# Loading a tile's queries by one transfer of 2 KB rows instead of two transfers of 1 KB rows

## The chip, the cores and the metric

The kernel runs on one core of one Trainium2 chip. The metric is device time in microseconds (us) for one execution. Three executions of the kernel before took 438.06, 438.45 and 440.13 us; their median, 438.45 us, is the time before. One further execution was profiled: 438.54 us, with a span of 436.9 us from its first to its last instruction.

## The reference

A decayed linear attention ("retention") is followed by a mixture of eight experts. `q`, `k` and `v` are fp32 arrays of 4 batches x 8 heads x 768 tokens x 64 values.

```python
for b in range(nb):                       # blocks of 64 tokens, in order
    intra = einsum('bhic,bhjc->bhij', qb, kb) * Dmask   # lam ** (i - j), i >= j
    intra = einsum('bhij,bhjd->bhid', intra, vb)
    inter = einsum('bhid,bhde->bhie', qb * lam_pow, kv_state)
    out[:, :, sl] = intra + inter
    kv_state = lam_block * kv_state + einsum('bhsd,bhse->bhde', kb_dec, vb)
# then, with x = the 3072 x 512 rows of out:
e_idx = argmax(x @ w_gate, axis=1)        # one expert per row
out[row] = gate * eom * (relu(x @ w1[e]) @ w2[e])
```

## The kernel before, in words

The work has two stages. In the first, the attention runs over 24 tiles: a tile is 128 tokens of one batch with all eight heads, and the four batches of one stretch of 128 tokens follow each other. In the second, the rows are gathered expert by expert and go through `w1` and `w2`.

For a tile `n`, `load_qkv` (line 145) brings three blocks of 256 KB from HBM, all issued by SP (SyncE): the keys in two transfers (line 171), the queries in two (line 165), the values in one (line 173). Keys and values land with one token per partition, so their contiguous pieces are one head's 64 values, 256 bytes. The queries land in another way: a partition holds four successive tokens of one head, 1 KB that is contiguous in HBM. One transfer brings heads 0 to 3 into columns 0 to 255 of the tile, the other heads 4 to 7 into columns 256 to 511. Partition `4s + m` of the first holds tokens `4s` to `4s+3` of head `m`.

`stage_a` (line 312) turns keys and queries over on TensorE: four 128x128 transposes of the keys into the PSUM bank `pk`, four of the queries into `pq` (line 325). ScalarE then copies `pk` to `kT` in one instruction (line 328) and `pq` to `qT` in four, each of 64 partitions x 256 elements (line 330). It is these four copies that put the tokens back in order: `query_parts` (line 303) gives for each copy the elements of `pq` it reads and the places in `qT` it writes, every second column. After `stage_a`, `qT` has the same layout whatever way the queries came in. `stage_b` (line 347) multiplies `kT` and `qT` into the banks `ps`, VectorE applies the decay (line 368), `stage_c1` and `stage_c` multiply with the running state (line 383) and with the values (line 400) and update the state (line 413). ScalarE takes the result to `xT` (line 407), VectorE turns it to rows `xn` (line 475), and SP writes those to the DRAM buffer `x_d` (line 477), from which the experts gather later (line 769).

The order of the instructions on each engine is the order of the code (a schedule written out by hand). In step `s` of the loop at line 1054, SP is given the keys and queries of a tile five to seven steps ahead, the values of a tile two less ahead, and then the `x_d` write of tile `s - 1`; GpSimd (POOL) forms `qd` (line 339) and the decayed keys `kd` (line 300). Tiles 0 to 15 land in eight buffers that the expert weights use later; those of tiles 18 to 21 land in a shared pool of 44 slots, which also holds `kT`, `qT`, `xT` and `xn`. A slot that held `xn` is free when its `x_d` write has landed. SP works through its transfers in that order, one after the other, with nothing else in between.

The pieces of the code that the steps below touch:

Of the kernel before, what the change touches and what calls it, by code (L numbers as in the profile page):

```python
# [23 lines left out]
def kernel(  # L24
# [13 lines left out]
    nc = tc.nc  # L38
    B, H, S, D = q.shape
# [3 lines left out]
    NPAIR = H // 2  # L43
# [31 lines left out]
    def slot(name, dtype=F32):  # L75
        return pool.tile([P, 512], dtype, tag="slot", bufs=NSLOT, name=name)
# [68 lines left out]
    def load_qkv(n, i0=0, i1=3):  # L145
        if n >= NTILE:
            return
        c, b = divmod(n, B)
        ts = qkv.setdefault(n, [])
        if n not in packs:  # L150
            if n < EARLY + 2:
                tag, bufs = (("whi", 4), ("wlo", 4))[n % 2] if n < EARLY else ("raw", 3)
                t = wpool.tile([P, 4, 512], F32, tag=tag, bufs=bufs, name=f"qkv_{n}")
                packs[n] = [t[:, i, :] for i in range(4)]
            elif n >= NTILE - 2:
                ts2 = [pool.tile([P, 8 * P], F32, tag="wide", bufs=4, name=f"qkv_{n}_{i}") for i in range(2)]
                packs[n] = [t[:, 512 * i : 512 * i + 512] for t in ts2 for i in range(2)]
        for i, (nm, src) in list(enumerate((("k", k), ("q", q), ("v", v))))[i0:i1]:
            t = packs[n][i] if n in packs else slot(f"{nm}_{n}")
            rows = src[b, :, c * P : (c + 1) * P, :]  # L160
            if nm == "q":

                rows = rows.rearrange("(y m) (s r) d -> y s m (r d)", y=2, r=4)
                for j in range(2):
                    nc.sync.dma_start(t[:, 256 * j : 256 * j + 256], rows[j])
            else:
                t = t.rearrange("p (h d) -> p h d", h=H)
                rows = rows.rearrange("h t d -> t h d")
                if nm == "k":
                    for y in range(2):  # L170
                        nc.sync.dma_start(t.rearrange("p (m y) d -> p y m d", y=2)[:, y], rows[:, 4 * y : 4 * y + 4])
                else:
                    nc.sync.dma_start(t, rows)
            ts.append(t)


    with tc.manual_schedule():
        lamb = const.tile([P, H], F32, name="lamb")
        nc.scalar.dma_start(lamb, lam.rearrange("(o h) -> o h", o=1).broadcast_to([P, H]))
        load_qkv(0, 0, 2)  # L180
        blank = const.tile([P, 512], BF16, name="blank")
        nc.gpsimd.memset(blank, 0.0)
        warm = const.tile([P, 1], F32, name="warm")
        nc.gpsimd.memset(warm, 0.0)
        idle = bank("idle")

        def keep_warm(count):
            for _ in range(count):
                nc.tensor.matmul(idle, blank[:, 0:P], blank, start=True, stop=True)

        keep_warm(7)
        nc.scalar.activation(out=warm, in_=warm, func=AF.Exp)
        ident = const.tile([P, P], F32, name="ident")
        make_identity(nc, ident)
        decay = pool.tile([P, H, P], F32, tag="decay", name="decay")
        load_qkv(1, 0, 2)
        wgs = const.tile([P, NKC, EG], F32, name="wgs")
        nc.gpsimd.memset(wgs, 0.0)
        load_qkv(0, 2, 3)
        for n in range(2, AHEAD):  # L200
            load_qkv(n, 0, 2)
            if n == 2:
                nc.sync.dma_start(wgs[:, :, 0:E], w_gate.rearrange("(c p) e -> p c e", p=P))
                nc.sync.dma_start(wgs[:, :, E : 2 * E], w_output_gate.rearrange("(c p) e -> p c e", p=P))
            else:
                load_qkv(n - 2, 2, 3)
# [96 lines left out]
    def query_parts(pq):  # L303
        for j in range(2):
            for o in range(2):
                yield (
                    slice(j * D, (j + 1) * D),
                    lambda t, o=o: t.rearrange("p g (s i o) -> p g s i o", i=2, o=2)[:, :, :, :, o],
                    pq[o * D : (o + 1) * D, 256 * j : 256 * j + 256].rearrange("p (i s g) -> p g s i", i=2, g=NPAIR),
                )  # L310

    def stage_a(n):
        c, b = divmod(n, B)
        k_in, q_in = qkv[n][0:2]
        pk = bank(f"pk_{n}")
        pq = bank(f"pq_{n}")
        for src, dst in ((k_in, pk), (q_in, pq)):
            if n < 2 and (n > 0 or dst is pq):
                keep_warm(1)
            if dst is pq:  # L320
                src = src.rearrange("p (m y d) -> p m y d", y=2, d=D)
            else:
                src = src.rearrange("p (m y) d -> p m y d", y=2)
            for m in range(4):
                nc.tensor.transpose(out=dst[:, m * P : (m + 1) * P], in_=src[:, m], identity=ident)  # L325
        kT = slot(f"kT_{n}").rearrange("p (g t) -> p g t", g=NPAIR)
        qT = slot(f"qT_{n}").rearrange("p (g t) -> p g t", g=NPAIR)
        nc.scalar.copy(out=kT, in_=pk.rearrange("p (g t) -> p g t", g=NPAIR))
        for r, view, src in query_parts(pq):
            nc.scalar.copy(out=view(qT[r]), in_=src)  # L330
        live[n] = dict(kT=kT, qT=qT, qd=None, kd=None)
# [708 lines left out]
    with tc.manual_schedule():  # L1040
# [181 lines left out]
        for p in range(E):  # L1222
# [3 lines left out]
            rows = p not in TURNED  # L1226
# [41 lines left out]
            for i, j in enumerate(steps):  # L1268
# [10 lines left out]
                m = max(ns - 1, 1)  # L1279
# [108 lines left out]
```

## Time and profile before

| | |
|---|---|
| Median of three executions | 438.45 us (438.06 to 440.13) |
| Profiled execution, its span | 438.54 us, 436.9 us |
| TensorE busy (matmul) | 401.5 us, 92% of the span |
| VectorE, ScalarE, GpSimd busy | 285.5, 188.0, 235.7 us |
| Transfers issued by SP's queue | 88240 packets, 62.40 MB |
| First and last issue of queries by SP | 1.9 us, 98.6 us |

The attention stage fills about the first 120 us: the last copy to `qT` starts at 119.7 us. In the rows of the trace, PE is TensorE, DVE is VectorE, ACT is ScalarE, POOL is GpSimd, SPq is the queue of SP in which it issues transfers; L165 is line 165 of the kernel. "DMA share" is the mean busy share of the 16 engines that carry the transfers, 1.00 when all 16 have a packet under way all the time. A busy TensorE is not a TensorE at its peak, since matmuls are pipelined.

### The profile page before, as it was taken

How to read it: one execution, taken by the hardware profiler on the slowest of the kernel's cores; microseconds unless marked ns; L12 is line 12 of the kernel's file. 1: busy time of each engine (PE TensorE's matmuls, PEld its weight loads, DVE VectorE, ACT ScalarE, POOL GpSimd, SP SyncE). 2: the span in 40 equal slices, each digit the busy share in tenths (PEclk: the TensorE clock that was granted, in tenths of full speed). 3: DMA queues.
4: the chain of work that ended last, by engine and by line, in shares of the span. 5: the costliest groups of instructions: out<-in, count | busy, mean ns of one | idle time of the engine just before them, and what ended most of it. 6: DMA issues, size and time to landing. Idle time of an engine off the chain costs nothing.

```text
span 436.9 us, 10421 instructions
## 1 busy us (share of the span) xinstructions
PE 401.5 (92%) x3816; PEld 366.4 (84%) x3816; DVE 285.5 (65%) x822; ACT 188.0 (43%) x455; POOL 235.7 (54%) x284
## 2 busy tenths in 40 slices
PE   8999899788366989979999999999999999999993
PEld 4888789677355969669999999999999989989983
DVE  3757768394587853485967966886785774874610
ACT  5766576355423602254604613532642552542400
POOL 4276866655485287758668366366376446311011
PEclk9999999999695999999999999999999999999998
DMA  7989898989672135565447945965964876361001
GB/s 171 219 241 242 213 249 215 246 227 263 188 216 76 49 95 203 160 199 183 132 158 209 298 144 170 290 220 151 292 221 131 266 247 216 128 202 60 1 28 50
DMA packets 95471, 79.42 MB, mean 182 GB/s; under 512 B 59564, under 2 KB 71856, under 8 KB 95408
## 3 DMA queue, kind: packets, MB, share of 16 engines
q1 hardware_dynamic: 88240, 62.40, 48.8%
q0 software_dynamic: 7024, 16.24, 11.9%
q8 instruction: 32, 0.52, 0.5%
q14 instruction: 31, 0.25, 0.2%
q10 hardware_dynamic: 144, 0.00, 0.0%
HBM read 62.45 MB, written 16.55 MB: 181 GB/s over the span
## 4 chain that ended last, share of the span: by engine, by line
PE 68%; DMA 11%; DVE 8%; SPq 4%; issue 4%; POOL 3%; ACT 1%; POOLq 0%; DVEq 0%; ACTq 0%
PE ph_None L80 9%; PE ph_None L81 9%; PE ph_None L79 9%; PE py L79 5%; PE py L81 5%; PE py L80 5%; DMA xg<-x_d,rows 4%; PE pyr L80 3%; PE pyr L79 3%; PE pyr L81 3%; PE po L400 3%; PE ps L359 2%; DMA index<-tab_d 2%; DMA qkv<-in_k_dram 2%; DVE wlo L133 2%
## 5 line engine op out<-in xcount | busy, mean ns | idle before, releaser
L769 POOL DMA_INDIRECT xg<-x_d,rows x103 | 114.2, 1109 | 77.3 <-issue 32.3
L133 DVE TENSOR_TENSOR wlo<-raw,whi 128x512 fp32r<-128x512 f32 x128 | 87.7, 708 | 0.6 <-ACT whi L124 0.6
L836 ACT ACTIVATE hhi<-ph_None 128x400 fp32r<-128x400 f32 (+4 forms) x56 | 28.1, 501 | 116.9 <-PE ph_None L81 112.1
L79 PE MATMUL ph_None<-xhi,whi 128*128 128x400 f32 (+4 forms) x224 | 76.3, 341 | 2.2 <-ACT xhi L800 2.2
L80 PE MATMUL ph_None<-xlo,whi 128*128 128x400 f32 (+4 forms) x224 | 76.3, 341 | 0.3 <-DVE xlo L804 0.3
L81 PE MATMUL ph_None<-xhi,wlo 128*128 128x400 f32 (+4 forms) x224 | 76.2, 340 | 0.0
L124 ACT CAST whi<-raw 128x512 fp32r<-128x512 f32 x128 | 74.4, 615 | 3.1 <-DMA raw<-in_moe_w_dram 3.1
L837 DVE SCALAR_TENSOR_TENSOR hlo<-ph_None,hhi 128x400 fp32r<-128x400 f32 (+4 forms) x56 | 31.8, 567 | 33.9 <-ACT hhi L836 31.9
L368 DVE TENSOR_TENSOR at<-ps,decay 128x512 f32<-128x512 f32 x48 | 31.5, 686 | 27.0 <-PE ps L359 21.7
L79 PEld LDWEIGHTS ph_None<-xhi,whi 128*128 128x128 f32 x224 | 42.0, 188 | 3.1 <-ACT xhi L800 2.7
L80 PE MATMUL py<-hlo,whi 128*128 128x400 f32 (+2 forms) x128 | 44.5, 348 | 0.0
L81 PE MATMUL py<-hhi,wlo 128*128 128x400 f32 (+2 forms) x128 | 44.5, 348 | 0.0
L79 PE MATMUL py<-hhi,whi 128*128 128x400 f32 (+2 forms) x128 | 44.5, 348 | 0.0
L80 PEld LDWEIGHTS ph_None<-xlo,whi 128*128 128x128 f32 x224 | 42.1, 188 | 1.0 <-DVE xlo L804 0.6
L81 PEld LDWEIGHTS ph_None<-xhi,wlo 128*128 128x128 f32 x224 | 42.1, 188 | 0.3
L330 ACT COPY qT<-pq 64x256 f32<-64x256 f32 x96 | 37.6, 391 | 7.5 <-PE pq L325 6.6
L953 POOL DMA_INDIRECT out_dram<-yn,table x12 | 12.7, 1058 | 49.9 <-DVE yn L1013 32.6
L81 PE MATMUL pyr<-whi,hlo 128*128 128x512 f32 (+2 forms) x96 | 37.5, 391 | 0.2 <-DVE hlo L837 0.2
L80 PE MATMUL pyr<-wlo,hhi 128*128 128x512 f32 (+2 forms) x96 | 37.5, 391 | 0.0
L79 PE MATMUL pyr<-whi,hhi 128*128 128x512 f32 (+2 forms) x96 | 37.5, 390 | 0.0
L800 ACT CAST xhi<-y 128x256 fp32r<-128x256 f32 (+3 forms) x64 | 19.8, 362 | 38.7 <-DVE y L786 30.3
L612 POOL DMA_INDIRECT tab_d<-rec,idx x24 | 24.9, 1039 | 18.7 <-issue 11.2
(179 smaller groups left out, 762.3 us busy)
## 6 DMA issues: line engine op xcount, KB each, us to landing
raw<-in_moe_w_dram SPq DMA_DIRECT2D x29, 1024.0 KB
qkv<-in_k_dram SPq DMA_DIRECT2D x40, 128.0 KB
qkv<-in_q_dram SPq DMA_DIRECT2D x40, 128.0 KB
qkv<-in_v_dram SPq DMA_DIRECT2D x20, 256.0 KB
x_d<-xn SPq DMA_DIRECT2D x20, 256.0 KB
raw<-in_moe_w_dram POOLq DMA_DIRECT2D x3, 1024.0 KB, 5.8
yd<-yo SPq DMA_DIRECT2D x12, 256.0 KB
yr<-yd SPq DMA_DIRECT2D x48, 64.0 KB
```

What stands on the lines that cost most here:

```text
L79: nc.tensor.matmul(ps, a[0], b[0], start=first, stop=False)
L80: nc.tensor.matmul(ps, a[0], b[1], start=False, stop=False)
L81: nc.tensor.matmul(ps, a[1], b[0], start=False, stop=last)
L124: nc.scalar.copy(out=hi, in_=src)
L133: eng.tensor_tensor(out=lo, in0=src, in1=hi.bitcast(F32), op=ALU.subtract)
L330: nc.scalar.copy(out=view(qT[r]), in_=src)
L368: nc.vector.tensor_tensor(out=at, in0=ps.rearrange("p (g t) -> p g t", g=NPAIR), in1=dec[:, j], op=ALU.mult)
L612: nc.gpsimd.indirect_dma_start(out=tab_d, out_offset=bass.IndirectOffsetOnAxis(ap=idx, axis=0), in_=rec, in_offset=None, bounds_check=P * ...
L769: nc.gpsimd.indirect_dma_start(out=xg[(p, b // 4)][:, (b % 4) * P : (b % 4 + 1) * P], out_offset=None, in_=x_q[0 : 4 * rows], in_offset=ba ...
L800: nc.scalar.copy(out=hi, in_=src)
L836: nc.scalar.activation(out=hi[:, r], in_=ph[:, r], func=AF.Relu)
L837: nc.vector.scalar_tensor_tensor(out=lo[:, r], in0=ph[:, r], scalar=0.0, in1=hi[:, r].bitcast(F32), op0=ALU.max, op1=ALU.subtract,)
```

## The change

The two transfers become one. A partition now holds eight successive tokens of one head, 2 KB that is contiguous in HBM: partition `16h + s` holds tokens `8s` to `8s+7` of head `h`. The source is walked as 8 heads, 16 pieces in each, 512 elements in each piece; before it was 32 pieces, 4 heads, 256 elements, once for each half of the heads. The transposes are the same four instructions; what their columns mean is different, and so `query_parts` reads `pq` in another order. The copies remain four of 64x256 and write the same elements of `qT` in the same order, every second column.

```diff
             if nm == "q":
 
-                rows = rows.rearrange("(y m) (s r) d -> y s m (r d)", y=2, r=4)
-                for j in range(2):
-                    nc.sync.dma_start(t[:, 256 * j : 256 * j + 256], rows[j])
+                nc.sync.dma_start(t, rows.rearrange("h (s r) d -> h s (r d)", r=8))
...
             for o in range(2):
                 yield (
                     slice(j * D, (j + 1) * D),
-                    lambda t, o=o: t.rearrange("p g (s i o) -> p g s i o", i=2, o=2)[:, :, :, :, o],
-                    pq[o * D : (o + 1) * D, 256 * j : 256 * j + 256].rearrange("p (i s g) -> p g s i", i=2, g=NPAIR),
+                    lambda t, o=o: t.rearrange("p g (s m o) -> p g s m o", m=4, o=2)[:, :, :, :, o],
+                    pq[o * D : (o + 1) * D].rearrange("p (m y g s) -> p y g s m", m=4, y=2, g=NPAIR)[:, j],
                 )
```

On TensorE, VectorE, ScalarE and GpSimd the instructions stand in the same order and number. On SP, 24 transfers are gone. The head of SP's queue, before (the number behind `qkv` is the buffer of a tile; the last figures are partitions and elements, and `x2` stands for two equal transfers):

```order
L171 DMA qkv_78<-in_k_dram 128x4x64 x2
L165 DMA qkv_78<-in_q_dram 128x1x256 x2
L171 DMA qkv_102<-in_k_dram 128x4x64 x2
L165 DMA qkv_102<-in_q_dram 128x1x256 x2
L173 DMA qkv_78<-in_v_dram 128x8x64
```

and now (the lines stand two higher, and the buffers have other numbers):

```order
L169 DMA qkv_78<-in_k_dram 128x4x64 x2
L163 DMA qkv_78<-in_q_dram 128x1x512
L169 DMA qkv_101<-in_k_dram 128x4x64 x2
L163 DMA qkv_101<-in_q_dram 128x1x512
L171 DMA qkv_78<-in_v_dram 128x8x64
```

Nothing changes places; everything behind a tile's queries comes one transfer earlier for each tile ahead of it. Further on, in step 6, where the keys and queries of two tiles are issued together, before:

```order
L171 DMA qkv_808<-in_k_dram 128x4x64 x2
L165 DMA qkv_808<-in_q_dram 128x1x256 x2
L171 DMA qkv_813<-in_k_dram 128x4x64 x2
L165 DMA qkv_813<-in_q_dram 128x1x256 x2
L173 DMA qkv_571<-in_v_dram 128x8x64
L173 DMA qkv_700<-in_v_dram 128x8x64
L477 DMA x_d<-xn_873 128x512
```

and now:

```order
L169 DMA qkv_797<-in_k_dram 128x4x64 x2
L163 DMA qkv_797<-in_q_dram 128x1x512
L169 DMA qkv_801<-in_k_dram 128x4x64 x2
L163 DMA qkv_801<-in_q_dram 128x1x512
L171 DMA qkv_562<-in_v_dram 128x8x64
L171 DMA qkv_690<-in_v_dram 128x8x64
L475 DMA x_d<-xn_860 128x512
```

The values of tiles 9 and 10 and the `x_d` write stand behind two query transfers in place of four.

## The prediction

> **What bounds the kernel now.** I read first the windows by stage, to see which stage the queries' transfers lie in and whether another could give time back. Columns are the stretch, its length, the busy time of each engine, the granted TensorE clock, the mean busy share of the 16 transfer engines, and GB/s.
>
> ```profile
> 0.00:22.00 22.00, 19.48 (x274) 14.45 (x274) 11.96 (x36) 13.94 (x33) 7.65 (x42) 1.00 0.83 195
> 22.00:82.00 60.00, 56.33 (x1246) 49.84 (x1245) 42.05 (x147) 35.08 (x94) 42.91 (x45) 1.00 0.89 233
> 82.00:110.00 28.00, 22.84 (x500) 19.47 (x498) 15.01 (x53) 15.55 (x43) 14.68 (x15) 1.00 0.93 248
> 0.00:110.00 110.00, 98.65 (x2016) 83.76 (x2016) 69.02 (x234) 64.58 (x170) 65.24 (x101) 1.00 0.89 229
> 140.00:436.90 296.90, 284.99 (x1573) 268.10 (x1570) 194.31 (x515) 112.94 (x255) 152.09 (x164) 0.99 0.52 167
> ```
>
> From 140 us on TensorE works 285.0 of 296.9 us: a delay of the attention reaches the end undiminished, and time won there is won at the end. In the first 110 us two resources are near full together: TensorE, 98.65 us, and the transfer engines, 0.89 x 110 = 97.9 us, so 12.1 us are free on the average transfer engine.
>
> Next the timeline of SP's queue, its start and one steady piece (start, length, line, transfers).
>
> ```profile
> 0.92 0.99 SPq L171 DMA_DIRECT2D qkv<-in_k_dram  x2
> 1.95 1.29 SPq L165 DMA_DIRECT2D qkv<-in_q_dram  x2
> 3.28 1.14 SPq L171 DMA_DIRECT2D qkv<-in_k_dram  x2
> 4.46 1.19 SPq L165 DMA_DIRECT2D qkv<-in_q_dram  x2
> 5.69 0.60 SPq L173 DMA_DIRECT2D qkv<-in_v_dram  x1
> ...
> 34.06 1.90 SPq L171 DMA_DIRECT2D qkv<-in_k_dram  x2
> 36.01 1.21 SPq L165 DMA_DIRECT2D qkv<-in_q_dram  x2
> 37.26 0.59 SPq L173 DMA_DIRECT2D qkv<-in_v_dram  x1
> 37.95 0.52 SPq L477 DMA_DIRECT2D x_d<-xn  x1
> 38.57 1.92 SPq L171 DMA_DIRECT2D qkv<-in_k_dram  x2
> ```
>
> SP issues without a pause; a tile took it 38.57 - 34.06 = 4.5 us there, of which the two query transfers are 1.2. So SP is a third full resource. What this costs is in the table of waits (engine and line, what it waited for, total, times, longest), for 0 to 110 us, and in the long steps of the chain that ended last:
>
> ```profile
> POOL kd L300 <- DMA qkv<-in_k_dram: 4.7, 1, 4.7
> PE po L400 <- DMA qkv<-in_v_dram: 3.0, 2, 1.9
> ACT xT L407 <- DMA x_d<-xn: 2.0, 1, 2.0
> ACT kT L328 <- DMA x_d<-xn: 1.7, 1, 1.7
> PE pq L325 <- DMA qkv<-in_q_dram: 0.6, 2, 0.5
> PE pk L325 <- DMA qkv<-in_k_dram: 0.4, 1, 0.4
> ```
>
> ```profile
> 17.19 5.10 DMA qkv<-in_k_dram
> 31.88 4.71 DMA qkv<-in_q_dram
> 77.55 5.26 DMA x_d<-xn
> 106.52 7.41 DMA index<-tab_d
> ```
>
> TensorE waits only 3.0 + 0.6 + 0.4 = 4.0 us for transfers in 110, but each of k, q, v and the `x_d` write stands in the chain at some point: they arrive just in time, with no stock. Whatever slows transfers is felt soon.
>
> **The change, part by part.** *The issues.* 48 query transfers become 24. A query transfer holds SP for 0.60 us, a key transfer for 0.56:
>
> ```profile
> L165 SPq DMA_DIRECT2D qkv<-in_q_dram x40: 540/602/1788, 1.9 to 98.6; - x40
> L171 SPq DMA_DIRECT2D qkv<-in_k_dram x40: 367/558/1826, 0.9 to 97.1; - x40
> ```
>
> 24 x 0.60 = 14.4 us of SP's time go. What they are worth depends on whether SP can use them: at the start it can, since the engines are still empty. Tile 1's keys, for which POOL waits 4.7 us, are behind one query issue fewer, tile 2's behind two: I take the latter, 2 x 0.65 = 1.3 us of the start. Later the gain has a ceiling, the 4.0 us of TensorE's waits, and is had only if the transfers themselves do not become slower.
>
> *The transfers.* They do, I think. The bytes are the same, 256 KB a tile. But the outermost count of the source falls from 32 to 8, while every other large load of SP has an outermost count that is a multiple of 16 (128 partitions). How a transfer is dealt out shows in the ACT queue's single transfer, the 128 rows of `lamb`:
>
> ```profile
> q10 hardware_dynamic: 144, 0.00, 0.0%
> lamb<-in_lam_dram ACTq DMA_DIRECT2D x1, 4.0 KB
> ```
>
> 144 packets are 128 rows and 16 more, one for each engine, so its outer rows were dealt to all 16. Eight outer rows can be dealt to no more than eight engines unless they are cut further, which no row here shows. My forecast is that the new query transfer runs on eight.
>
> The Trainium skill ("DMA: Bandwidth & Descriptors", section "Why a DMA increments its semaphore by 16 and not by 1") says that the number of engines is the largest one up to 16 that divides the slowest dimension of both sides, and that the queue of SP takes the lowest-numbered ones. By that rule it is 8, always the same eight; no run here has shown a transfer with fewer than 16, and without the rule the sum would be that of the second rival.
>
> The price of a tile's queries on one engine, from two stretches in which the expert weights come in rows of 2 KB and more:
>
> ```profile
> 105.00:107.00 2.00, 1.28 (x48) 1.04 (x40) 0.00 (x0) 1.94 (x6) 0.00 (x0) 1.00 1.00 294
> 243.00:246.00 3.00, 3.00 (x17) 2.98 (x17) 2.83 (x7) 2.39 (x7) 0.00 (x0) 1.00 1.02 403
> ```
>
> Per engine that is 294 / 1.00 / 16 = 18.4 and 403 / 1.02 / 16 = 24.7 GB/s. 262144 bytes on eight engines then take 1.78 or 1.33 us, and I take 1.40, nearer to the fast end because half the engines leave memory to the others. Before, on 16 engines in 1 KB pieces, the dearest price is the average of the stage, 229 / 0.89 / 16 = 16.1 GB/s, or 1.02 us, the cheapest 24.7 GB/s, or 0.66; I take 0.75, since 1 KB lies nearer to 2 KB than to the 256-byte rows that make the average. Each of the eight loaded engines so gets 0.65 us more a tile, between 0.31 (1.33 - 1.02) and 1.12 (1.78 - 0.66). Over 24 tiles: 15.6 us, between 7 and 27. The other eight get less work, which helps nobody, because a transfer of keys or values has landed only when its last engine has.
>
> *The sum.* The loaded engines have 97.9 + 15.6 = 113.5 us of work where 110 were available: 3.5 us too much. They also cannot start before about 2 us, when the first packets follow the first issue at 0.92: 5.5. The start gains 1.3: +4.2, and of this a little is lent by packets that overlap (a share of 1.02 above), so +4.0. On the profiled run's 438.54 us this is 442.5; its distance to the median, 0.1 us, is nothing here. SP then waits for room in its queue instead of issuing, so the waits of TensorE for values and queries grow in place of shrinking, behind them `ps`, VectorE's decay and ScalarE's `xT`, which all follow TensorE; and the `x_d` writes, on whose landing ScalarE waits 3.7 us for free slots, come later too.
>
> *The copies.* ScalarE reads `pq` with the same large step (128 columns) innermost, four times in a row instead of twice, and writes as before. The nearest rows are the strided copies of today and a copy of the same length without a stride:
>
> ```profile
> L330 ACT COPY qT<-pq 64x256 f32<-64x256 f32 x96 | 37.6, 391 | 7.5 <-PE pq L325 6.6
> L407 ACT COPY xT<-po 128x256 f32<-128x256 f32 x48 | 16.8, 373 | 12.8 <-PE po L400 7.9 <-DMA x_d<-xn 2.0 <-PE pq L325 1.7
> ```
>
> All the striding costs 18 ns a copy, so a change of it is bounded by 96 x 0.018 = 1.7 us either way, on an engine that is busy 64.58 of 110 us: nothing. Without that cover, as in the few places where the chain runs through `qT`, it is 0.07 us a tile. The transposes have the same shapes: nothing.
>
> **The rivals.** *Eight engines, absorbed (same).* Break-even is where the added load fits into the 12.1 free us less the 2 of the start: 10.1 / 24 = 0.42 us a tile. That is inside my bounds (0.31 to 1.12): it holds if the old price was near 1.0, or if the two-fold shorter issue lets SP fill the gaps that the engines have today while queries are issued. For it: the free 12 us are an average and can be used. Against it: the chain's landings of 5 us show queues that already build up. It gives 438.5.
>
> *Sixteen engines (faster).* If the eight rows are cut further and dealt to all, the load stays (0.66 to 0.89 us a tile against 0.66 to 1.02) and SP's 14.4 us are a plain gain: TensorE's 4.0 us of waits go, and 1.3 of the start: 438.5 - 5.3 = 433 at best, 434.5 with some wait left. Against it is the count of 8.
>
> *Eight engines, and one of them already the last (much slower).* The engines carry more than data:
>
> ```profile
> q8 instruction: 32, 0.52, 0.5%
> ```
>
> 32 packets of 16 KB hold one engine each for some 0.66 us at 24.7 GB/s. TensorE has 2016 of its 3816 matmuls before 110 us, so about 17 of them, 11 us, fall there. If they go always to one engine, it has 97.9 + 11 = 109 of 110 us today, which would explain why single SP issues take up to 1.8 us. If that one is among the eight, no reserve is left: it decides from the first tile, and 15.6 - 1.3 - (1 free us) = 13 us would be lost, of which the slack between tiles may give back a few: 449.
>
> **How the numbers follow.** What a measurement of this kernel can tell from no change is 0.5%, 2.2 us: under 436.3 is faster, over 440.6 slower. Chances: forecast 0.48, with its own range 440 to 447; absorbed 0.22; sixteen engines 0.16; the last engine 0.14. Faster: 0.16 and 0.06 of the absorbed case, whose start may gain: 0.22. Same: the other 0.16 and 0.07 of the forecast's lower end: 0.23. Slower: 0.41 + 0.14 = 0.55. The time is that of the likeliest, 442.5. The range takes in sixteen engines as far as 434 and the last engine as far as 451.
>
> **What would show it.** In the section on queues, SP's queue has 88240 packets; 6144 of 1 KB give way to 3072 of 2 KB. If each engine that takes part adds one closing packet, 48 x 16 of these go, and 24 x 8 come with eight engines or 24 x 16 with sixteen: 84592 or 84784. The bytes stay at 62.40 MB. In the forecast the waits `po L400 <- in_v_dram` and those for `in_q_dram` and `in_k_dram` grow from 4.0 us to about 8, SP has issues of well over 0.6 us at the values and keys that follow queries, and the last `qT` copy starts near 124 us, not 119.7. If SP runs ahead, these waits vanish and the copy starts before 117, the transfers were not slowed, and the step on the eight engines is wrong. If `qT` takes other than 0.39 us, the step on the copies is. If the attention ends as forecast but the whole does not, the windows after 140 us will show that they gave time back, against what I read there.

## The result, and the profile after

The changed kernel took 441.31 us (median of six executions, 440.83 to 443.95), the kernel before 437.96 us beside it. The ratio is 1.0096, with a 95% interval of 1.0067 to 1.0125: 3.35 us slower, more than can be taken for no change. The profiled execution took 441.37 us, its span is 439.7 us against 436.9.

The windows by stage of the kernel after (columns as in the prediction):

```profile
0.00:22.00 22.00, 16.14 (x206) 10.77 (x206) 9.25 (x29) 11.39 (x27) 6.95 (x41) 1.00 0.83 163
22.00:82.00 60.00, 57.60 (x1262) 50.43 (x1266) 43.69 (x150) 38.35 (x101) 40.47 (x42) 1.00 0.96 233
0.00:110.00 110.00, 96.03 (x1918) 80.79 (x1919) 70.06 (x234) 63.34 (x164) 63.78 (x100) 0.98 0.92 215
140.00:439.70 299.70, 287.56 (x1589) 270.67 (x1585) 197.39 (x524) 113.34 (x257) 154.25 (x165) 0.99 0.52 166
```

Within 110 us 1918 matmuls are on record, not 2016, and 215 GB/s come in, not 229, while the transfer engines show *more* busy time: 0.92, not 0.89. The start is hurt most: in the same 22 us 163 GB/s instead of 195. The granted clock does not explain it: its mean is 0.976 over this execution and 0.977 over the one before, and up to 82 us it is 1.00 in both. After 140 us nothing is given back: TensorE works 287.6 of 299.7 us there, as densely as before.

SP's queue in the section on queues and, below it, its timeline at the start (start, length, line, transfers) after the change:

```profile
q1 hardware_dynamic: 84592, 62.39, 50.3%
```

```profile
0.92 1.00 SPq L169 DMA_DIRECT2D qkv<-in_k_dram  x2
1.97 0.78 SPq L163 DMA_DIRECT2D qkv<-in_q_dram  x1
2.79 0.96 SPq L169 DMA_DIRECT2D qkv<-in_k_dram  x2
3.79 0.64 SPq L163 DMA_DIRECT2D qkv<-in_q_dram  x1
4.47 0.46 SPq L171 DMA_DIRECT2D qkv<-in_v_dram  x1
4.97 2.31 SPq L169 DMA_DIRECT2D qkv<-in_k_dram  x2
7.33 2.76 SPq L163 DMA_DIRECT2D qkv<-in_q_dram  x1
```

84592 is the count that the prediction worked out for eight engines. For two tiles SP is ahead: the first values are issued at 4.47 us, before at 5.69. Then the keys of tile 2 hold SP for 2.31 us and its queries for 2.76 us, and the lead is gone. Nor did the lead bring anything earlier. The landings of the keys of tile 1 stand in both chains that ended last (start, length), first before, then after:

```profile
3.91 2.83 DMA qkv<-in_k_dram
```

```profile
3.25 4.79 DMA qkv<-in_k_dram
```

They were issued 0.66 us earlier and landed 1.30 us later, at 8.04 us and not at 6.74. The rows of single operations (minimum, median, maximum in ns, first and last start in us; the row of queries is without tiles 18 to 21) show that a long issue is no exception:

```profile
L163 SPq DMA_DIRECT2D qkv<-in_q_dram x20: 621/1396/2759, 2.0 to 102.2; - x20
L328 ACT COPY qT<-pq x96: 375/393/426, 7.7 to 122.9; 64x256 f32<-64x256 f32 x96
```

One issue of queries has a median of 1396 ns, more than the two of 602 ns that it replaces. Medians leave out the few long issues, though. Added up from the timelines, all 48 issues of queries before held SP for 34.7 us, the 24 after for 31.5: of the 14.4 us that were to be saved, 3.2 are. More than that goes at the `x_d` writes, whose issues come to 22.4 us instead of 14.7 (before, then after):

```profile
L477 SPq DMA_DIRECT2D x_d<-xn x22: 337/524/2117, 24.1 to 145.1; - x22
L475 SPq DMA_DIRECT2D x_d<-xn x22: 337/946/2499, 26.1 to 148.2; - x22
```

The copies are as long as before, and the last starts 3.2 us later (119.7 before).

The table of waits after the change, 0 to 110 us:

```profile
ACT kT L326 <- DMA x_d<-xn: 5.0, 2, 4.1
PE pq L323 <- DMA qkv<-in_q_dram: 4.9, 6, 1.4
ACT qT L328 <- DMA x_d<-xn: 3.8, 1, 3.8
ACT xT L405 <- DMA x_d<-xn: 1.7, 1, 1.7
PE po L398 <- DMA qkv<-in_v_dram: 0.8, 1, 0.8
PE pk L323 <- DMA qkv<-in_k_dram: 0.3, 1, 0.3
```

TensorE waits for transfers 4.9 + 0.8 + 0.3 = 6.0 us (4.0 before): for queries 4.9 instead of 0.6, for values 0.8 instead of 3.0. ScalarE, which needs the slots that an `x_d` write sets free, waits 5.0 + 3.8 + 1.7 = 10.5 us, where it was 3.7. Two landings of queries stand in the chain that ended last (start, length); the longest landing of queries in the chain before took 4.71 us:

```profile
23.38 6.64 DMA qkv<-in_q_dram
...
42.61 6.93 DMA qkv<-in_q_dram
```

How the delay grows is seen from when TensorE begins to turn over the keys of tiles 2, 5, 11, 17 and 23. The timeline of TensorE, first the kernel before, then after:

```profile
11.70 0.66 PE L325 MATMUL pk<-ident,qkv 128*128 128x128 f32 x4
...
22.43 0.63 PE L325 MATMUL pk<-ident,qkv 128*128 128x128 f32 x4 [0.38 <-DMA qkv<-in_k_dram]
...
49.19 0.66 PE L325 MATMUL pk<-ident,qkv 128*128 128x128 f32 x4
...
76.51 0.66 PE L325 MATMUL pk<-ident,qkv 128*128 128x128 f32 x4
...
115.82 1.09 PE L325 MATMUL pk<-ident,qkv 128*128 128x128 f32 x4 [7.28 <-issue]
```

```profile
13.79 0.66 PE L323 MATMUL pk<-ident,qkv 128*128 128x128 f32 x4
...
25.21 0.66 PE L323 MATMUL pk<-ident,qkv 128*128 128x128 f32 x4
...
54.47 0.66 PE L323 MATMUL pk<-ident,qkv 128*128 128x128 f32 x4
...
80.07 0.66 PE L323 MATMUL pk<-ident,qkv 128*128 128x128 f32 x4
...
118.95 1.09 PE L323 MATMUL pk<-ident,qkv 128*128 128x128 f32 x4 [4.83 <-issue]
```

The attention is late by 2.1, 2.8, 5.3, 3.6 and 3.1 us. The first two microseconds are lost before tile 2; what is lost in the middle comes back in part; some 3 us reach the end.

### The profile page after: what moved, and what is told of

It is laid out like the page before. It is cut to its first block, busy times and chain, and to the rows that moved or that the text cites. A ratio compares the mean times of both kernels' runs of the same rounds, so it can differ in the third digit from the quotient of the medians.

```text
span 439.7 us, 10409 instructions
## 1 busy us (share of the span) xinstructions
PE 402.7 (92%) x3816; PEld 366.5 (83%) x3816; DVE 286.5 (65%) x822; ACT 188.9 (43%) x455; POOL 235.8 (54%) x284
## 3 DMA queue, kind: packets, MB, share of 16 engines
q1 hardware_dynamic: 84592, 62.39, 50.3%
## 4 chain that ended last, share of the span: by engine, by line
PE 65%; DMA 15%; DVE 7%; SPq 5%; POOL 3%; issue 3%; ACT 1%; POOLq 0%; DVEq 0%; ACTq 0%
PE ph_None L80 9%; PE ph_None L81 9%; PE ph_None L79 9%; PE py L80 5%; PE py L79 5%; PE py L81 5%; PE pyr L80 3%; PE pyr L79 3%; PE pyr L81 3%; DMA xg<-x_d,rows 3%; DMA qkv<-in_q_dram 3%; DMA qkv<-in_v_dram 3%; DMA tab_d<-rec,idx 2%; SPq L169 2%; PE po L398 2%
## 5 line engine op out<-in xcount | busy, mean ns | idle before, releaser
L366 DVE TENSOR_TENSOR at<-ps,decay 128x512 f32<-128x512 f32 x48 | 31.5, 685 | 30.2 <-PE ps L357 26.0
L951 POOL DMA_INDIRECT out_dram<-yn,table x12 | 12.7, 1055 | 49.9 <-DVE yn L1011 32.7
```

The source lines that it names most:

```text
L366: nc.vector.tensor_tensor(out=at, in0=ps.rearrange("p (g t) -> p g t", g=NPAIR), in1=dec[:, j], op=ALU.mult)
```

## The experiments

The theory: the query transfer runs on eight engines, and that costs the time. Against it stood that the number of engines does nothing and something else in the change costs: fewer but longer issues, the 2 KB rows, the walk of one engine through one head. The kernel before took 438.0 us beside the change, and 445.3, 448.1, 447.3 and 449.0 us in the four comparisons that follow, so only ratios to the kernel before, run beside each, are compared. Where a ratio is set against an expected time, it is taken times 438 us.

All variants differ in the walk of the query transfer, and in `query_parts`, which reads `pq` in the order that fits. The diffs show the walk; only the first shows the order of `pq` too.

**Sixteen engines, one transfer of 2 KB rows (one_on_16).** Against the changed kernel:

```diff
-                nc.sync.dma_start(t, rows.rearrange("h (s r) d -> h s (r d)", r=8))
+                nc.sync.dma_start(t, rows.rearrange("h (s r) d -> s h (r d)", r=8))
...
-                    pq[o * D : (o + 1) * D].rearrange("p (m y g s) -> p y g s m", m=4, y=2, g=NPAIR)[:, j],
+                    pq[o * D : (o + 1) * D].rearrange("p (m s y g) -> p y g s m", m=4, y=2, g=NPAIR)[:, j],
```

> The changed kernel with one thing different: the 16 pieces of a head are walked outermost and the heads inside them (partition 8s + h in place of 16h + s), so the source's outermost count is 16, not 8. Rows of 2 KB, one transfer a tile and the number of copies stay. Theory 'eight engines': the loss goes and SP's shorter queue is left as a gain, 433.5 to 436.5 us, 84784 packets in SP's queue (24 x 8 closing packets more than the change's 84592), a query issue of SP near 0.6 us again. Rival 'one transfer': if it is the single transfer or the 2 KB row that costs, whatever the number of engines, about 441. Rival 'copies': ScalarE's copies stay at 0.39 us in both; if the order in which they read costs, the time stays over 440 while the waits for queries go.

Measured: 442.53 us against 445.34, ratio 0.9945 (0.9904 to 0.9985). The packets, one issue of queries, the copies, the waits and the windows of this kernel:

```profile
q1 hardware_dynamic: 84784, 62.40, 51.3%
```

```profile
L163 SPq DMA_DIRECT2D qkv<-in_q_dram x20: 542/997/2862, 2.0 to 95.8; - x20
L328 ACT COPY qT<-pq x96: 374/391/411, 7.1 to 117.6; 64x256 f32<-64x256 f32 x96
```

```profile
PE pq L323 <- DMA qkv<-in_q_dram: 2.2, 3, 1.0
```

```profile
0.00:110.00 110.00, 99.06 (x1983) 83.24 (x1987) 70.57 (x234) 64.99 (x170) 65.18 (x101) 0.98 1.02 231
```

84784 packets are 24 x 16 closing ones instead of 24 x 8. Same bytes, same rows, same number of issues, two loops exchanged: the loss of 1.0% becomes a gain of 0.55%. That is 435.6 us, inside the range that was expected; a query issue near 0.6 us was expected too, and its median is 1.00. The last copy starts at 117.6 us, TensorE waits 2.2 us for queries instead of 4.9. The walk on eight engines thus costs 1.0096 / 0.9945 = 1.015 against the one on sixteen. Which piece of HBM an engine reads changed with it; that is taken apart further down. This kernel beats both others.

**Two transfers of 1 KB rows, on eight engines and on four (two_on_8, two_on_4).** Against the kernel before, one edit each:

```diff
-                rows = rows.rearrange("(y m) (s r) d -> y s m (r d)", y=2, r=4)
+                rows = rows.rearrange("h (y s r) d -> y h s (r d)", y=2, r=4)      # two_on_8
```

```diff
-                rows = rows.rearrange("(y m) (s r) d -> y s m (r d)", y=2, r=4)
+                rows = rows.rearrange("(y m) (s r) d -> y m s (r d)", y=2, r=4)    # two_on_4
```

> The kernel before with the two transfers kept, 1 KB rows kept, but each transfer takes 64 tokens of all eight heads with the head outermost: outermost count 8, not 32. Theory 'eight engines': the same load on half the engines as in the change, without SP's saving: 441 to 445 us, packets 88240 - 48 x 8 = 87856. Rival 'one transfer': as before, 438.

> The kernel before with the walk of each transfer turned round, heads outermost (4) and pieces inside: partition 32m + s in place of 4s + m. Theory 'eight engines' as a law of load: four engines, a tile's queries take 2.8 us on each in place of 0.75, 24 x 2.05 = 49 us more on top of 97.9, so 147 + 2 - 110 = 39 us lost: about 477 us (465 to 482), 88240 - 48 x 12 = 87664 packets. If the loss of the change comes from the latency of the first tiles alone, some 6 us: 444. Rival 'one transfer': 438.

Measured on eight: 1.0054 (1.002 to 1.0089), and in a later comparison (two_on_8_again, below) 1.005; 1.0054 is 440.4 us, just under the 441 to 445 that were expected. Measured on four: 472.96 us against 445.34, 27.6 us slower where 39 were expected, one timed execution. The packet counts, 87856 and 87664, are 48 x 8 and 48 x 4 closing packets where there were 48 x 16. The queue, waits and windows of the kernel on four engines:

```profile
q1 hardware_dynamic: 87664, 62.39, 44.5%
```

```profile
PE pq L325 <- DMA qkv<-in_q_dram: 13.6, 14, 1.4
...
PE po L400 <- DMA qkv<-in_v_dram: 5.9, 2, 3.4
```

```profile
0.00:110.00 110.00, 86.61 (x1604) 69.97 (x1604) 55.51 (x186) 52.05 (x133) 53.91 (x89) 0.94 0.68 175
```

With two transfers of 1 KB rows throughout, on sixteen, eight and four engines, the cost goes 0, 0.5, 6.2%. On four engines the mean busy share falls to 0.68 while TensorE waits 13.6 us for queries: on the mean the engines stand idle for a third of the time, and still the queries come late. A mean share does not show what a few engines carry.

**The start alone and the rest alone (start_on_8, later_on_8).** Tiles 0 to 5 head by head on eight engines, the others on sixteen, and the reverse; one transfer of 2 KB rows for all:

```diff
-                nc.sync.dma_start(t, rows.rearrange("h (s r) d -> h s (r d)", r=8))
+                walk = "h (s r) d -> h s (r d)" if n < 6 else "h (s r) d -> s h (r d)"   # start_on_8; later_on_8: n >= 6
+                nc.sync.dma_start(t, rows.rearrange(walk, r=8))
```

> Tiles 0 to 5 as in the change (heads outermost), tiles 6 to 23 as in the run with 16 outermost pieces. Where is the time lost? If the load adds up over all tiles (the prediction's sum), only a quarter of it is there and SP makes it good later: within 1 us of the run with 16 pieces throughout. If it is lost at the start, where TensorE of the changed kernel is already 2.8 us late at tile 5, and never made good: 2 to 4 us above that run.

> The counterpart of the run with tiles 0 to 5 on eight engines: here tiles 6 to 23 have the head outermost, tiles 0 to 5 have 16 pieces outermost. With tiles 0 to 5 alone on eight engines nearly nothing was lost (ratio 0.996 against 0.9945). Theory 'the load adds up over the tiles': this run has most of the loss, 1.004 to 1.010. Rival 'the start must come first' (the start uses up the stock, and only then the later tiles cost): it stays below 1.000.

Measured: start_on_8 0.9958 (0.9918 to 0.9998), later_on_8 1.0019 (0.9983 to 1.0054). The timeline of TensorE at tiles 5 and 23, of one_on_16 and then of start_on_8:

```profile
22.96 0.66 PE L323 MATMUL pk<-ident,qkv 128*128 128x128 f32 x4
...
113.63 0.63 PE L323 MATMUL pk<-ident,qkv 128*128 128x128 f32 x4 [1.70 <-issue]
```

```profile
24.96 0.66 PE L325 MATMUL pk<-ident,qkv 128*128 128x128 f32 x4
...
113.59 0.63 PE L325 MATMUL pk<-ident,qkv 128*128 128x128 f32 x4 [1.62 <-issue]
```

The start on eight engines is 2.0 us late at tile 5, and on time again at tile 23: sixteen engines make it good. That is what the load that adds up had forecast for start_on_8. For later_on_8 neither theory came out: 1.0019 lies between the 1.004 to 1.010 of the one and the 1.000 of the other, and its interval reaches both. Against one_on_16 the start costs 0.1%, the later tiles 0.7%, all tiles 1.5%. That the whole is more than the two parts would fit a delay that can be caught up only where there is room left, but with intervals of 0.4% either way the excess is not shown.

**Are the saved issues the gain (change_again, spare_issue)?** The changed kernel once more, so that it stands beside the others; and one_on_16 with a small second transfer issued behind each one of queries, whose bytes nobody uses:

```diff
+    spare_q = const.tile([P, 2 * NTILE], F32, name="spare_q")
...
+                nc.sync.dma_start(spare_q[0:16, 2 * n : 2 * n + 2], rows[0, 0:16, 0:2])
```

> The changed kernel once more, beside the kernel before and the two runs below on one chip, since the run with two transfers on eight engines lost only 0.54% and the run with one transfer on sixteen gained 0.55%. If costs add (engines +0.54%, one transfer -0.55%), the change should stand at 1.000; if they do not add, at 1.008 to 1.011 as it first did: then a single 256 KB transfer on eight engines costs more than two of 128 KB on the same eight.

> The kernel with one transfer on sixteen engines, and behind each query transfer a second one of 16 pieces of 8 bytes into a place that nothing reads, so that SP issues as many transfers as in the kernel before. Theory 'SP's queue': the gain of one transfer on sixteen engines came from SP's 24 issues, and is gone: 0.999 to 1.003. Rival 'row length': 2 KB rows are what gains: it stays at 0.993 to 0.997.

Measured: change_again 1.0101 (1.0058 to 1.0143). spare_issue 1.0018 (0.9981 to 1.0055). The row of the added transfer and the row of the queries in spare_issue:

```profile
L164 SPq DMA_DIRECT2D spare_q<-in_q_dram x24: 577/586/1673, 2.7 to 100.2; - x24
```

```profile
L163 SPq DMA_DIRECT2D qkv<-in_q_dram x20: 547/664/2238, 2.0 to 98.5; - x20
```

An issue that brings next to nothing holds SP 0.59 us, 24 of them 14 us, and the gain of 0.55% is gone. That speaks for SP's time as the source of the gain on sixteen engines; the intervals touch (0.9985 and 0.9981), and the added transfers put packets on the transfer engines as well, so it isn't proved. change_again also answers another question: were the costs independent, the changed kernel would be two_on_8 times one_on_16, 1.0054 x 0.9945 = 1.000. It is 1.010.

**Is it the single transfer or the row length (two_2k_on_8, two_on_8_again)?** Two transfers again, each of 64 partitions in rows of 2 KB, head by head:

```diff
-                rows = rows.rearrange("(y m) (s r) d -> y s m (r d)", y=2, r=4)
+                rows = rows.rearrange("h (k s r) d -> k h s (r d)", k=2, r=8)
...
-                    nc.sync.dma_start(t[:, 256 * j : 256 * j + 256], rows[j])
+                    nc.sync.dma_start(t[64 * j : 64 * j + 64], rows[j])
```

> Eight engines and rows of 2 KB as in the change, but in two transfers, each 64 tokens of all eight heads (64 partitions, head outermost). The change stood at 1.0096 and 1.0101, two transfers on eight engines with rows of 1 KB at 1.0054, though SP has fewer issues in the change. If it is the one large transfer that costs more on eight engines (nothing is issued behind it until all its rows have found room), this run is near 1.005. If it is the 2 KB row on eight engines, it is near 1.010, or over it, since SP's two issues are kept.

> Two transfers on eight engines, rows of 1 KB, once more, beside the run above: 1.005 again. If it comes out near 1.010, there is nothing to tell apart between it and the change, and the loss is that of eight engines alone.

Measured: two_2k_on_8 1.0141 (1.0098 to 1.0183), two_on_8_again 1.005 (1.002 to 1.008). The windows of the two in that order, then the queries' wait of two_2k_on_8 and of two_on_8_again:

```profile
0.00:110.00 110.00, 93.94 (x1828) 78.41 (x1829) 66.15 (x227) 59.78 (x155) 61.68 (x98) 0.97 0.93 208
```

```profile
0.00:110.00 110.00, 98.70 (x1891) 82.10 (x1893) 70.06 (x233) 62.69 (x163) 64.39 (x101) 0.96 0.87 220
```

```profile
PE pq L325 <- DMA qkv<-in_q_dram: 5.4, 7, 1.7
```

```profile
PE pq L325 <- DMA qkv<-in_q_dram: 2.1, 3, 0.9
```

That one transfer is dearer than two falls: two are no cheaper. On eight engines 2 KB rows are dearer than 1 KB rows by 0.9%. The edit has a second difference, though, 64 partitions to a transfer; and all eight-engine kernels so far let one engine read one head in a piece, while all on sixteen read scattered rows.

**The walk, and 2 KB rows on sixteen engines (two_2k_8_walk, two_2k_on_16).** The first differs from two_2k_on_8 only in the order of the walk; the second is the kernel before with 2 KB rows in 64 partitions:

```diff
-                rows = rows.rearrange("h (k s r) d -> k h s (r d)", k=2, r=8)
+                rows = rows.rearrange("h (k s r) d -> k s h (r d)", k=2, r=8)       # two_2k_8_walk
```

```diff
-                rows = rows.rearrange("(y m) (s r) d -> y s m (r d)", y=2, r=4)
+                rows = rows.rearrange("(y m) (s r) d -> y s m (r d)", y=2, r=8)     # two_2k_on_16
...
-                    nc.sync.dma_start(t[:, 256 * j : 256 * j + 256], rows[j])
+                    nc.sync.dma_start(t[64 * j : 64 * j + 64], rows[j])
```

> Two query transfers of 64 partitions and 2 KB rows on eight engines, as in two_2k_on_8, but with the token groups outermost (8 of them) and the heads inside: each engine then reads eight scattered rows of 2 KB where in two_2k_on_8 it read 16 KB of one head in one piece. All eight-engine kernels so far walked one head per engine, all sixteen-engine ones walked scattered rows, so the walk has not been told apart from the count. Theory, the count of engines costs: 1.014 again (1.009 to 1.019). Rival, one engine's reading from one place costs: as sixteen engines, 1.000 (0.996 to 1.004). Packets 84784 in both.

> Two query transfers of 64 partitions and 2 KB rows, one of each half of the heads, on sixteen engines (16 token groups outermost). Beside the kernel before only the row is longer and a transfer fills 64 partitions, not 128. Theory, long rows cost only where eight engines carry them: 1.000 (0.996 to 1.004). Rival, the 64 partitions are what made two_2k_on_8 dearer than two_on_8: 1.009 (1.005 to 1.013). Packets 88240 - 3072 = 85168 in both.

Measured: two_2k_8_walk 1.0123 (1.0076 to 1.017), two_2k_on_16 0.997 (0.9934 to 1.0005). Their queues, in that order:

```profile
q1 hardware_dynamic: 84784, 62.40, 49.4%
```

```profile
q1 hardware_dynamic: 85168, 62.40, 47.6%
```

Scattered rows on eight engines cost what rows in one piece cost, so the walk is not the cause of what these two lose. 64 partitions and 2 KB rows on sixteen engines cost nothing, so neither of these is by itself. What is left is the count of engines, alone (two_on_8) or together with one of them: whether two_2k_on_8 is dearer than two_on_8 by its rows or by its 64 partitions, these runs do not tell apart. The change has the long rows on 128 partitions and is dearer than two_on_8 too, though its interval touches that of two_on_8. All ratios together:

| query transfers of a tile | 16 engines | 8 engines | 4 engines |
|---|---|---|---|
| two, 1 KB rows | 1 (the kernel before) | 1.0054, 1.005 | 1.062 (one execution) |
| two, 2 KB rows, 64 partitions each | 0.997 | 1.0141, 1.0123 | |
| one, 2 KB rows | 0.9945 | 1.0096, 1.0101 (the change) | |

Each step to the right costs. Read down, the second row costs 0.8% over the first on eight engines and nothing on sixteen, and joining the two transfers gives 0.3% on either, which is within the intervals.

One sum goes along with these ratios: how long SP was held by all its issues of keys, queries, values and `x_d` writes, in us, added up from the timelines of the profiled executions, in the same places:

| query transfers of a tile | 16 engines | 8 engines | 4 engines |
|---|---|---|---|
| two, 1 KB rows | 95.0 | 96.1, 97.8 | 122.4 |
| two, 2 KB rows, 64 partitions each | 92.6 | 101.0, 103.2 | |
| one, 2 KB rows | 93.1 | 100.3, 102.2 | |

Four engines hold SP 27.4 us longer, and the kernel is 27.6 us slower; the change holds it 5.3 us longer for 3.35, one_on_16 1.9 us less for a gain of 2.4. In spare_issue the sum is 95.2 us, as before. Up to 104 us SP is issuing for 92.7 us in the kernel before, so there is little slack in which a longer issue could hide. The start alone on eight engines (start_on_8) has 93.9 us at 0.9958; the rest alone (later_on_8) fits worst, 98.7 us at 1.0019. The sums are of one execution each and do not prove the direction, but they fit an SP that sets the pace of the attention and is held when the transfer engines fall behind.

## Why the prediction was right or wrong

**Eight engines: right.** The packets are 84592 to the packet, and six variants give the counts that follow from the outermost loop. The Trainium skill's rule in "DMA: Bandwidth & Descriptors" (section "Why a DMA increments its semaphore by 16 and not by 1"), that the count of engines is the largest one up to sixteen that divides the slowest dimension, gave the right number each time, for sixteen, eight and four; that they are the lowest-numbered ones no run here shows.

**What that costs: right in sign, somewhat high in size.** The prediction set 442.5 for eight engines and 434.5 for sixteen, 8 us apart. Measured on the scale of 438 us, it is 0.0151 x 438 = 6.6 us, with the two cases at 442.2 and 435.6. The term "15.6 us over 24 tiles", 0.65 us a tile, can be worked back: of 3.35 us the wait for the first packets takes 2, the free time is 12.1, and with no gain at the start (3.35 - 2 + 12.1) / 24 = 0.56 us are left. That is an estimate in the terms of the sum, and lies inside its bounds. The packets in the traces agree with the prices taken: in SP's queue those of 1 KB have a median of 46 ns before, those of 2 KB 84 ns after (up to 24 us, where they are queries alone). A tile has 16 of them on an engine, 0.74 us and 1.34 us, where the prediction took 0.75 and 1.40. That holds for medians: the means up to 24 us are 57 and 122 ns, which would give 0.91 and 1.95 us. On four engines the same working gives (27.6 - 2 + 12.1) / 24 = 1.57 us, where its expectation had put 2.05. With rows of 1 KB on eight engines it gives (2.4 - 2 + 12.1) / 24 = 0.52 us, a third of that, and an engine has a third of the added bytes: like for like the load follows the bytes, at a lower price than expected.

**"The start gains 1.3": wrong in sign.** It was the term that failed: it counted an earlier issue as an earlier landing. The shorter program of SP did show for two tiles (values issued at 4.47 us, not 5.69), but the keys of tile 1 landed 1.30 us later; then SP was held 2.31 and 2.76 us at tile 2, and TensorE took up that tile 2.1 us late. On sixteen engines it took it up at about the time of before:

```profile
12.07 0.66 PE L323 MATMUL pk<-ident,qkv 128*128 128x128 f32 x4
```

12.07 us against 11.70: no gain there either. In the total the failed term and the load that was set too high nearly cancelled: +4.0 us forecast, +3.35 measured. The rest of the 1.2 us between 441.31 and 442.5 is the kernel before, which took 437.96 us beside the change and not the 438.54 that the sum starts from.

**SP's stalls: right that they come, wrong in place.** The prediction had them "at the values and keys that follow queries". They are at the queries themselves, 1396 ns for one, and at the `x_d` writes. All issues of keys come to 32.2 us where they came to 30.8, those of values to 14.1 where they came to 14.8: there the change hardly shows. So the 14.4 us saved at 24 issues of 0.60 us were not there to be used: 3.2 us were saved at the queries, 7.7 lost at the `x_d` writes. On sixteen engines the queries come to 24.9 us, so 9.8 are saved there; part of the saving stays, and spare_issue suggests that this is the gain.

**Waits: right in direction, less than said, and elsewhere.** TensorE's waits for transfers grew from 4.0 to 6.0 us, not to 8; those for values, which were to grow, fell from 3.0 to 0.8, those for queries rose from 0.6 to 4.9. The slow transfer itself is what comes late, not only what queues behind it. That `x_d` writes come later was right, and larger than thought: ScalarE's 3.7 us became 10.5.

**The end: right.** The last copy starts at 122.9 us (forecast near 124), 3.2 us later than before, the time is 3.35 us longer, and the windows after 140 us gave nothing back. **The copies: right**, 393 ns against 392.

**That bytes and their price decide: wrong, and covered by luck.** The prediction took 2 KB rows as a little cheaper by the byte than 1 KB rows, and packet by packet they are (84 ns and 2 x 46). Yet on eight engines the kernels with 2 KB rows are the slower ones: two transfers stand at 1.0132 in the mean with rows of 2 KB, at 1.0052 with rows of 1 KB. Eight engines with 1 KB rows cost 0.0054 x 438 = 2.4 us, and one transfer on sixteen engines gains 2.4 us; had the two simply added, the change would have cost nothing. So the 3.35 us measured hold an effect on eight engines, of the long rows as it seems, that the sum does not contain, and that the time came out near is in part luck.

**The rivals.** Absorbed fell with the time itself and with one_on_16: the load isn't hidden. Sixteen engines was no description of this change, but one_on_16 is that case, and its gain is 0.0055 x 438 = 2.4 us where the rival had 4. One engine already the last would have cost 10.5 us, the change cost 3.35, and even on four engines the loss was below the expectation. Whether the eight engines hold the one that loads instructions, the runs don't say.

**What stays open.** Why the kernels with 2 KB rows lose more than those with 1 KB rows on eight engines, and not on sixteen. Where it costs is seen with two transfers: the issues of queries hold SP for 40.8 and 42.2 us there, for 32.7 and 32.1 with 1 KB rows on eight engines, and for 33.8 with 2 KB rows on sixteen. The view gives only the mean over sixteen engines, not what each one carries; a queue of long packets on the loaded eight, ahead of keys and values, would fit the higher share at fewer GB/s (0.93 at 208 against 0.87 at 220), but one_on_16 has the highest share of all, 1.02 at 231, and is the fastest. Single transfers with 1 KB rows on eight engines weren't tried, nor two transfers of 2 KB rows on 128 partitions.

## What to carry to other kernels

Before two transfers are joined, look at the outermost loop of the new walk: it sets how many engines share the bytes, and where that falls below sixteen the loss can exceed all that fewer issues bring. Then see whether the same bytes can be walked with another loop outermost: here the exchange of two loops and a view in the copies that follow turned a 1% loss into a 0.5% gain. Count the closing packets of the queue in the profile to see how many engines a transfer had; a mean busy share doesn't show it. And add up what the issuing engine is held for by all its transfers, before and after: in these runs that sum followed the time in the main, while the count of issues times the median of one did not.

## What the runs showed of the hardware that was not expected

- An issue is not a fixed cost. The same instruction for queries took from 0.54 to 2.86 us of SP in one kernel (one_on_16), and its median was 0.60 us for half a tile, 1.00 for a whole on sixteen engines, 1.40 on eight. With two transfers of 2 KB rows on eight engines the median stayed at 0.63 us (two_2k_8_walk), while all 48 issues together came to 42.2 us, where they came to 34.7 before, so a median can hide what the long ones cost:

```profile
L165 SPq DMA_DIRECT2D qkv<-in_q_dram x40: 598/628/2467, 2.0 to 107.1; - x40
```

- A transfer of 128 bytes in all, 16 rows of 8, holds SP as long as one of 128 KB: 586 against 602 ns.
- The busy share of the transfer engines rises where kernels get slower (0.92 at 215 GB/s after the change, 0.89 at 229 before) and where they get faster (1.02 at 231 in one_on_16), and falls to 0.68 where the bound is a few of them. By itself it tells neither the room left nor the bound.
